# Last output tile of an attention-and-ReGLU kernel: blocks of 256, 128, 64 and 64 columns from a ring of six PSUM banks

## Chip, cores, metric

One core of one Trainium2 chip. The metric is the device time of one execution in microseconds.

## The reference

```python
# x: 8 x 8 x 512 x 64, state: 8 x 8 x 32 x 64 (batch, head, rows, depth), float32
scores = x @ state^T / 8;  a  = softmax(scores);   xread = a @ state
scores2 = state @ x^T / 8; a2 = softmax(scores2);  sread = a2 @ x
y = concatenate([xread, sread], axis=rows)      # 8 x 8 x 544 x 64
t = y.transpose(0, 2, 1, 3).reshape(4352, 512)
out = (relu(t @ w_gate) * (t @ w_val)) @ w_out  # d_ff 1536, out 4352 x 512 float32
```

## The kernel before

Operands are bfloat16, sums are float32 in PSUM. Six banks (0 to 5) are a ring for most work, and two (6 and 7) hold output tiles in turn. An output tile has 128 rows of 512 columns and is the sum of 12 matmuls (`NF` = 12). It is copied from PSUM to one of four output buffers in SBUF and stored from there. At the very end come the two tiles of the state rows, row group 2 of the last batch and, as last tile, its row group 3, which `out_last` splits into column blocks.

```python
opool = pool("opool", 4)                # four output buffers, in turn
# ...
def bank(name, kind="r"):
    if given:
        n = given.pop(0)
    # ...
    else:
        n = turn["r"] % 6 if kind == "r" else 6 + turn["o"] % 2
        turn[kind] += 1
    return psum.tile([128, 512], FP32, name=name, tag=f"b{n}")

def o_bank():
    return bank("o_ps", "o")
# ...
def fin_x(b, tsub, eng="act"):
    o_sb = opool.tile([128, d_model], FP32, name="o_sb", tag="o_sb")
    copy[eng](out=o_sb, in_=held["o", b, tsub])
    n = 2 if b == B - 2 or (b == B - 1 and tsub == 0) else 1
    # ... n stores by SyncE
# ...
def out_last(b, tsub):
    for lo, n, eng, q in ((0, 256, nc.scalar.copy, nc.scalar), (256, 128, nc.scalar.copy, nc.scalar),
                          (384, 128, nc.vector.tensor_copy, nc.sync)):
        cols = slice(lo, lo + n)
        ps = o_bank()[:, 0:n]
        for jf in range(NF):
            nc.tensor.matmul(ps, hsb[b][:, jf, tsub * 128:(tsub + 1) * 128], wo_sb[:, jf, cols],
                             start=(jf == 0), stop=(jf == NF - 1))
        o_sb = opool.tile([128, d_model], FP32, name="o_sb", tag="o_sb")
        eng(out=o_sb[:, 0:n], in_=ps)
        q.dma_start(out=out_rows(b, tsub)[:, cols], in_=o_sb[:, 0:n])
# ...
for t2 in range(2):                      # state rows
    out_mms(hs_sb, B, t2, list(range(NF)))
    fin_s(t2)
for i in range(NF - lag % NF, NF - 3):   # row group 2 of the last batch
    out_piece(B - 1, i)
out_last(B - 1, NC - 1)
```

The softmax here doesn't subtract the row's maximum and nothing guards it: scores larger than these inputs give would overflow.

Of the kernel before, what the change touches and what calls it, by code (L numbers as in the profile page):

```python
# [16 lines left out]
def kernel(  # L17
# [9 lines left out]
    nc = tc.nc  # L27

    B, H, S, D = x.shape
# [51 lines left out]
# [4 lines that stand above are left out]
        elif kind == "spare":  # L85
            n = 6 + turn["o"] % 2
# [4 lines that stand above are left out]
# [255 lines left out]
    def o_bank():  # L346
        return bank("o_ps", "o")
# [8 lines left out]
    def out_rows(b, tsub):  # L356
        return out[b * SP: b * SP + S].rearrange("(p q) m -> q p m", q=NC)[tsub]

    def fin_x(b, tsub, eng="act"):
        o_sb = opool.tile([128, d_model], FP32, name="o_sb", tag="o_sb")  # L360
        copy[eng](out=o_sb, in_=held["o", b, tsub])  # L361
        n = 2 if b == B - 2 or (b == B - 1 and tsub == 0) else 1
        for i in range(n):
            rows = slice(128 // n * i, 128 // n * (i + 1))
            nc.sync.dma_start(out=out_rows(b, tsub)[rows], in_=o_sb[rows])
# [8 lines left out]

    def out_last(b, tsub):

        for lo, n, eng, q in ((0, 256, nc.scalar.copy, nc.scalar), (256, 128, nc.scalar.copy, nc.scalar),
                              (384, 128, nc.vector.tensor_copy, nc.sync)):
            cols = slice(lo, lo + n)
            ps = o_bank()[:, 0:n]  # L380
            for jf in range(NF):
                nc.tensor.matmul(ps, hsb[b][:, jf, tsub * 128:(tsub + 1) * 128], wo_sb[:, jf, cols],  # L382
                                 start=(jf == 0), stop=(jf == NF - 1))
# [3 lines that stand above are left out]
# [5 lines left out]
    def out_piece(b, i):  # L392
        out_part(b, i)
        if i % 3 == 2:
            fin_x(b, i // 3)
# [37 lines left out]
    def spin(n, cols=512):  # L433
        for i in range(n):
# [6 lines left out]
             "sc": att_sc, "ex": att_exp, "nr": att_sum, "nx": att_scale, "aT2": att_T2, "ao2": att_out2, "aT": att_T, "ao": att_out,  # L441
             "c": c_unit, "co": c_out, "u": u_unit, "uo": u_out, "gv": gv, "re": relu, "mu": mult, "o": out_part,
             "of": fin_x, "xn": x_next, "xp": x_pad, "sr": sr_mm, "sn": sr_norm}
    program = """
    dx.1.0.2 dx.1.1.2 stc.0.0.act stc.0.1.act xc.0.0.dve dw.0.0.128 spin.7 stT.0@4 xc.0.1.act dw.1.0.128 on xT.0.0@2
# [86 lines left out]
    for g in range(first, NF * (B + 1)):  # L532
        b, jf = divmod(g, NF)
# [14 lines left out]
    for i in range(NF - lag % NF, NF - 3):  # L548
        out_piece(B - 1, i)
    out_last(B - 1, NC - 1)  # L550


# [28 lines left out]
```

## Time and profile before

| What | Before |
|---|---|
| Time, median of the first 3 runs | 223.4 us (223.28 to 224.25) |
| Span of the profiled run, from the trace | 221.73 us |
| First matmul of the last tile (called T0 below) | 215.95 us |
| Tail: from T0 to the end of the span | 5.78 us |

The prediction shows the lines of the profile that matter and reads them. For reading them: SPq, ACTq and DVEq are the instruction queues of SyncE, ScalarE and VectorE, "landing" is the time from a store's issue to the signal that its data has arrived, and the chain that ended last is the work and waits followed back from the last instruction.

### The profile page before, as it was taken

To read this page: it belongs to the slowest core of one execution; us is meant where nothing else is said; L and a number is where in the kernel's file an instruction comes from. 1 tells how busy PE (TensorE), PEld (TensorE's weight loads), DVE (VectorE), ACT (ScalarE), POOL (GpSimd) and SP (SyncE) were. 2 spreads that over 40 slices of the span, in tenths; PEclk is the share of its full clock that TensorE was granted. 3 is DMA by queue.
4 is the path that set the end of the run, shared out by engine and by line. 5 is a ranking of instruction groups with operands and counts; after the bars stand their busy time and mean duration, and the time that the engine had idled before them with its cause. 6 is when DMAs were issued, how large, how long until landed. Compare 5 with 4: busy or idle time off the path is not lost.

```text
span 221.7 us, 4851 instructions
## 1 busy us (share of the span) xinstructions
PE 216.0 (97%) x1959; PEld 106.3 (48%) x1959; DVE 130.5 (59%) x228; ACT 124.8 (56%) x238; POOL 49.4 (22%) x54
## 2 busy tenths in 40 slices
PE   7799999999999999999999999999999999999994
PEld 3454455444554444444444444445444445666544
DVE  2697898965786569664767378646874433222100
ACT  5489888565767555564466456645654444222222
POOL 8777826460004233015000700000000000000000
PEclk9999999999999999999999999999999999999999
DMA  6999999182065962771169114501311112222332
GB/s 156 174 195 197 203 237 276 43 154 86 4 146 188 146 233 79 156 240 51 50 146 278 53 47 101 104 34 50 95 50 47 49 47 50 50 47 55 89 95 95
DMA packets 37879, 25.48 MB, mean 115 GB/s; under 512 B 18944, under 2 KB 33280, under 8 KB 37856
## 3 DMA queue, kind: packets, MB, share of 16 engines
q1 hardware_dynamic: 24992, 16.85, 28.7%
q0 software_dynamic: 11968, 7.47, 21.7%
q10 hardware_dynamic: 896, 0.85, 1.4%
q8 instruction: 15, 0.25, 0.5%
q14 instruction: 8, 0.07, 0.1%
HBM read 18.35 MB, written 8.91 MB: 123 GB/s over the span
## 4 chain that ended last, share of the span: by engine, by line
PE 85%; DMA 12%; POOL 1%; issue 0%; DVE 0%; POOLq 0%; DVEq 0%
PE o_ps L353 39%; PE gv_ps L316 32%; DMA xb<-in_x_dram 9%; PE gv_ps L333 5%; PE up L291 4%; DMA wg_sb<-in_moe_w_gate_dram 4%; PE sr_ps L264 1%; PE sc_ps L200 1%; PE o_ps L382 1%; PE xT_ps L186 0%; POOL xb L415 0%; PE stT_ps L129 0%; PE aT_ps L235 0%; PE srT_ps L277 0%; PE upc L291 0%
## 5 line engine op out<-in xcount | busy, mean ns | idle before, releaser
L353 PE MATMUL o_ps<-wo_sb,h_sb 128*128 128x512 bf16 x372 | 94.8, 379 | 0.0
L316 PE MATMUL gv_ps<-ans,U 128*128 128x512 bf16 x384 | 94.4, 379 | 0.0
L344 DVE TENSOR_TENSOR h_sb<-gv_ps,g_sb 128x512 bf16<-128x512 f32 x96 | 65.0, 689 | 43.5 <-ACT g_sb L340 42.1
L340 ACT ACTIVATE g_sb<-gv_ps 128x512 bf16<-128x512 f32 (+1 forms) x108 | 62.9, 588 | 45.9 <-PE gv_ps L316 35.0
L316 PEld LDWEIGHTS <-U 128*128 128x128 bf16 x384 | 36.1, 98 | 40.7 <-issue 0.4
L353 PEld LDWEIGHTS <-h_sb 128*128 128x128 bf16 x372 | 35.3, 98 | 39.7 <-issue 1.6
L361 ACT COPY o_sb<-o_ps 128x512 f32<-128x512 f32 x31 | 18.3, 590 | 17.4 <-PE o_ps L353 17.4
L301 ACT CAST U<-up 128x512 bf16<-128x512 f32 x36 | 18.9, 593 | 12.1 <-PE up L291 12.0
L142 POOL CAST xb<-xf 128x1024 bf16<-128x1024 f32 x10 | 10.6, 1088 | 66.4 <-DMA xf<-in_x_dram 45.4
L301 DVE CAST U<-up 128x512 bf16<-128x512 f32 x36 | 22.7, 684 | 4.1 <-PE up L291 3.7
L256 POOL COPY xa<-xb 128x2048 bf16<-128x2048 bf16 (+1 forms) x9 | 15.5, 1748 | 0.3
L213 DVE TENSOR_REDUCE cs<-e_sn 128x16 f32<-128x512 bf16 x16 | 10.9, 683 | 7.3 <-ACT e_sn L207 7.3
L344 DVE TENSOR_TENSOR hs_sb<-gv_ps,g_sb 128x256 bf16<-128x256 f32 x12 | 5.1, 425 | 15.3 <-PE gv_ps L333 10.8
L207 ACT ACTIVATE e_sn<-sc_ps 128x512 bf16<-128x512 f32 x16 | 9.6, 600 | 7.4 <-PE sc_ps L200 7.4
L219 DVE TENSOR_TENSOR a_sn<-e_sn,rc 128x512 bf16<-128x512 bf16 x16 | 12.4, 778 | 0.4
L291 PEld LDWEIGHTS <-stT 64*32 64x32 bf16 x512 | 5.9, 90 | 9.5 <-issue 8.1
L311 ACT CAST U<-upc 128x512 bf16<-128x512 f32 (+1 forms) x21 | 10.1, 570 | 0.5 <-PE upc L291 0.4
L200 PEld LDWEIGHTS <-xT 128*128 128x128 bf16 x128 | 5.7, 98 | 4.1 <-DVE xT L177 0.8
L291 PE MATMUL up<-wg_sb,stT 64*32 64x512 bf16 x144 | 7.5, 382 | 0.0
L291 PE MATMUL up<-wv_sb,stT 64*32 64x512 bf16 x144 | 7.2, 380 | 0.0
L333 PE MATMUL gv_ps<-br,wg_sb 128*128 128x256 bf16 x48 | 7.2, 273 | 0.0
L333 PE MATMUL gv_ps<-br,wv_sb 128*128 128x256 bf16 x48 | 7.2, 273 | 0.0
(63 smaller groups left out, 121.5 us busy)
## 6 DMA issues: line engine op xcount, KB each, us to landing
out_dram<-o_sb SPq DMA_DIRECT2D x26, 256.0 KB, 2.4
xf<-in_x_dram SPq DMA_DIRECT2D x4, 1024.0 KB, 6.3
wo_sb<-in_moe_w_out_dram POOLq DMA_DIRECT2D x2, 768.0 KB, 14.5
wg_sb<-in_moe_w_gate_dram POOLq DMA_DIRECT2D x5, 256.0 KB, 8.6
wv_sb<-in_moe_w_val_dram POOLq DMA_DIRECT2D x5, 256.0 KB, 10.5
out_dram<-o_sb SPq DMA_DIRECT2D x10, 128.0 KB, 2.4
xf<-in_x_dram POOLq DMA_DIRECT2D x1, 1024.0 KB, 16.1
xb<-in_x_dram POOLq DMA_DIRECT2D x3, 256.0 KB, 6.8
```

Source lines behind the costliest of these rows:

```text
L142: copy[eng](out=xb[b][:, :, hs].rearrange("p c h d -> p h c d"), in_=xf[b][:, hs])
L213: nc.vector.reduce_sum(out=cs, in_=e_v, axis=AX.X)
L219: {"dve": nc.vector, "pool": nc.gpsimd}[eng].tensor_tensor(out=by_pair(a_sn[b], jp).rearrange("p r (j n) -> p r j n", n=Ns), in0=e_v, in1= ...
L256: nc.gpsimd.tensor_copy(out=v[:, hs:hs + src.shape[1]], in_=src)
L291: nc.tensor.matmul(dst[parity][32 * j:32 * j + 32], stT[r:r + 64, b, j, 32 * parity:32 * parity + 32], wsb[r:r + 64, j, lo:lo + n], start= ...
L301: copy[eng](out=U[b][:, w, kc, lo:lo + 512], in_=held["u", b, w, lo][kc])
L316: nc.tensor.matmul(ps[w], U[b][:, w, kc, f0:f0 + 128], ANS[b][:, kc].rearrange("p c t -> p (c t)"), start=(kc == 0), stop=(kc == NK - 1))
L333: nc.tensor.matmul(ps[w][:, 0:nt], wsb[:, j, f0:f0 + 128], br[:, j].rearrange("p b n -> p (b n)"), start=(j == 0), stop=(j == NJ - 1))
L340: nc.scalar.activation(out=g_sb[:, 0:n], in_=ps[0][:, 0:n], func=AF.Relu)
L344: nc.vector.tensor_tensor(out=dst, in0=ps[1][:, 0:n], in1=held["g", b, jf][:, 0:n], op=ALU.mult)
L353: nc.tensor.matmul(held["o", b, tsub], src[:, jf, tsub * 128:(tsub + 1) * 128], wo_sb[:, jf], start=(jf == 0), stop=(jf == NF - 1))
L361: copy[eng](out=o_sb, in_=held["o", b, tsub])
```

## The change

The intent: a smaller last block gives a shorter last copy and a smaller last store. The four blocks come from the ring of six banks, so that no block waits for another's evacuation (its copy out of PSUM), and evacuations and stores are shared out. One earlier tile goes out in one store instead of two.

```diff
@@ fin_x
-        n = 2 if b == B - 2 or (b == B - 1 and tsub == 0) else 1
+        n = 2 if b == B - 2 else 1
@@ out_last
-        for lo, n, eng, q in ((0, 256, nc.scalar.copy, nc.scalar), (256, 128, nc.scalar.copy, nc.scalar),
-                              (384, 128, nc.vector.tensor_copy, nc.sync)):
+        for lo, n, eng, q in ((0, 256, nc.scalar.copy, nc.sync), (256, 128, nc.scalar.copy, nc.scalar),
+                              (384, 64, nc.vector.tensor_copy, nc.sync), (448, 64, nc.vector.tensor_copy, nc.scalar)):
             cols = slice(lo, lo + n)
-            ps = o_bank()[:, 0:n]
+            ps = bank("o_ps")[:, 0:n]
```

## The prediction

> **What bounds the kernel now.** I read the page first: busy shares and slices, then the chain that ended last. After that I read the pieces of that chain in the last microseconds, the instructions of the same stretch in order of time, and the landing times of the stores. The page says:
>
> ```profile
> PE 216.0 (97%) x1959; PEld 106.3 (48%) x1959; DVE 130.5 (59%) x228; ACT 124.8 (56%) x238; POOL 49.4 (22%) x54
> ...
> PEclk9999999999999999999999999999999999999999
> ...
> PE 85%; DMA 12%; POOL 1%; issue 0%; DVE 0%; POOLq 0%; DVEq 0%
> ```
>
> TensorE is busy for 97% of the span at full clock, and the chain is TensorE for 85%. Nothing but fewer or faster matmuls, or a shorter start or end, can move the time. The change touches only the end (and one store before it), so the end is all that needs sizing. The chain in order of time, from 205 us on, closes like this (start, duration, what):
>
> ```profile
> 207.48 8.63 PE o_ps L353 x40
> 216.11 2.67 PE o_ps L382 x36
> 218.78 0.04 DVEq L385
> 218.81 0.04 issue
> 218.85 0.29 DVE o_sb L385
> ```
>
> The 36 matmuls of the last tile follow the earlier ones without a gap, and the last block's evacuation on VectorE is the last work. The instructions of the tail in order of time (start, duration, engine, line; in brackets the idle time before and what ended it):
>
> ```profile
> 215.95 2.81 PE L382 MATMUL o_ps<-wo_sb,h_sb 128*128 128x256 bf16 x36
> 216.15 0.59 ACT L361 COPY o_sb<-o_ps 128x512 f32<-128x512 f32 x1 [2.00 <-PE o_ps L353]
> 216.76 0.35 SPq L365 DMA_DIRECT2D out_dram<-o_sb  x1
> 217.46 0.37 ACT L385 COPY o_sb<-o_ps 128x256 f32<-128x256 f32 x1 [0.72 <-PE o_ps L382]
> 217.86 0.36 ACTq L386 DMA_DIRECT2D out_dram<-o_sb  x1
> 218.39 0.27 ACT L385 COPY o_sb<-o_ps 128x128 f32<-128x128 f32 x1 [0.56 <-PE o_ps L382]
> 218.69 0.36 ACTq L386 DMA_DIRECT2D out_dram<-o_sb  x1
> 218.85 0.29 DVE L385 COPY o_sb<-o_ps 128x128 f32<-128x128 f32 x1 [10.84 <-PE o_ps L382]
> 219.17 0.35 SPq L386 DMA_DIRECT2D out_dram<-o_sb  x1
> ```
>
> The span ends at 221.7. After the last matmul that makes 0.07 us to the copy, 0.29 of copy, 0.03 to the store, and 2.56 from the start of the store's issue (219.17) to the end. The stores of this stretch:
>
> ```profile
> out_dram<-o_sb SPq DMA_DIRECT2D x2, 256.0 KB, 2.0
> out_dram<-o_sb SPq DMA_DIRECT2D x5, 64.0 KB, 1.7
> out_dram<-o_sb ACTq DMA_DIRECT2D x5, 64.0 KB, 2.0
> out_dram<-o_sb ACTq DMA_DIRECT2D x1, 128.0 KB, 1.9
> ```
>
> In a view of the last microseconds alone, both 64 KB stores of the last tile land after 1.6 us. So the last one lands at about 219.17 + 1.6 = 220.77, and some 0.96 us of closing semaphores and drains follow that no part of the change touches.
>
> **What the Trainium skill says.**
>
> (1) "PSUM — Partial Sum Buffer", section "PSUM bank collisions raise a hardware error": a bank that one engine writes must not be read by another at that moment, so TensorE must wait for the evacuation before it fills the bank again. Before, the three blocks alternate between two banks. The third reuses the bank of the first, whose copy ends at 217.46 + 0.37 = 217.83, and its first matmul starts at 217.93 by narrow windows of the timeline. There was 0.1 us to spare, and the view of that line lists no idle time of TensorE. So the bank wait that the ring of six would remove is not there in the kernel before.
>
> (2) "TensorE: Matmul & The Clock Gate", section "Back-to-back issue gap", gives about 81 ns per pair of weight load and matmul at 128 columns, and about 60 cycles (25 ns) as the floor up to 64 columns. The trace disagrees on the first: the starts of the 128-column matmuls run from 217.26 to 218.54 in 23 steps, 55.7 ns each. On the second it is close: the score matmuls (64 columns, a new 128x128 weight each) take 0.40 us for eight with 193 ns for one, so (0.40 - 0.193) / 7 = 29.6 ns a step:
>
> ```profile
> 150.11 0.40 PE L200 MATMUL sc_ps<-stT,xT 128*128 128x64 bf16 x8
> ```
>
> (3) "VectorE: DVE Perf Modes", section "The TRN2 errata", puts a copy from PSUM to SBUF at 120 + columns cycles of 0.96 GHz. For 128 columns that is 258 ns and the trace shows 292, so the fixed part is larger. The slope, 1.04 ns a column, agrees with the trace: the 512-column casts from PSUM take 684 ns, (684 - 292) / 384 = 1.02.
>
> (4) "DMA: Bandwidth & Descriptors", section "Anatomy of one DMA": most of a transfer's fixed 2 us is the receipt for the last byte. (It is stated for transfers issued by GpSimd; here stores from ScalarE and SyncE show 1.6 to 2.0.) So a fixed part remains however small the last store is.
>
> **The change part by part.**
>
> *One store instead of two for row group 0 of the last batch.* It goes out well before the tail, and saves one SyncE issue of about 0.35 us on a queue that mostly waits. Off the path: 0.
>
> *Ring of six banks.* It removes a wait of 0, as shown. It is needed by the other part, though: with two banks the fourth block would reuse the second's, whose copy ends at 218.39 + 0.27 = 218.66, while TensorE would want it at about 218.29.
>
> *The last 128 columns as two blocks of 64.* Twelve matmuls and weight loads more. The first starts at 217.93. 23 steps of 29.6 ns take the last one to 218.61, and with 193 ns it ends at 218.80, against 218.78 before: +0.02 us on the path. The last copy is 64 columns: 292 - 64 x 1.02 = 227 ns, so -0.065. It would begin at 218.87 and end at 219.10; plus 0.03, its store is ready at 219.13 (before 219.17).
>
> *Queues.* Block 0's store goes to SyncE, so ScalarE has only block 1's store (218.69) and then block 3's. Block 2's copy on VectorE starts at 217.93 + 11 x 0.0296 + 0.193 + 0.07 = 218.52, ends at 218.75 and its SyncE issue begins at 218.78, beside ScalarE's. Where both queues issued side by side in the tail, two issues took 0.85 us on ScalarE and 0.81 on SyncE, so about 0.43 each instead of 0.36. ScalarE is then free at 218.69 + 0.43 = 219.12, just before 219.13. The last issue starts at about 219.13: -0.04 in sum.
>
> *The last transfer.* Its rows are 256 bytes instead of 512. The trace's records of packets have about 27 ns for one of 512 bytes and 18 ns for one of 256 (in loads; no store of that size is in the trace). There are 128 rows over 16 engines, eight on each, so 8 x 9 = about 0.07 us less. I take 1.53 instead of 1.6 to landing, an estimate.
>
> *Sum.* TensorE +0.02, copy -0.065, queue 0, transfer -0.07: about -0.11 us of 223.4, 0.05%. That makes 223.3.
>
> **The rivals.**
>
> *The weight load, not the columns, sets the pace at 64 columns.* If each pair costs 55 ns as at 128 columns, the two blocks take 1.33 us instead of 0.66: +0.6 us, less the 0.14 of copy and transfer, so about 223.9. Against it speak the 29.6 ns above; for it, that those came in runs of eight and here 24 follow one another.
>
> *A buffer wait takes over.* Four output buffers go round. Block 3's copy takes the buffer of row group 2, whose 256 KB store is issued at 216.76 and lands 2.0 us later, at 218.76. TensorE releases the copy at 218.87. That is 0.1 us of margin. If that store lands 0.3 us late, the gain is gone and 0.2 is lost: 223.6.
>
> *ScalarE's queue serialises the last two stores.* It has only 0.01 us of margin in my own sum. If an issue beside another takes longer, or a semaphore instruction stands between, the last store starts up to 0.1 us late and the sum is 0: 223.4.
>
> *Short rows are slow to write.* "DMA: Bandwidth & Descriptors", section "Specifications", wants 512 bytes or more for line rate and says that shorter transfers make the engines read and write back. No store of this trace is that short. Some 0.2 us more on the landing would leave 223.5.
>
> **Range and chances.** All paths lie between 223.2 and 223.9, while the three runs before spread from 223.28 to 224.25. The spread of the runs is wider than the effect, so the range comes mainly from it: 223.3 us, 222.8 to 223.9 eight times in ten. Two per cent are 4.5 us, more than the 2.9 us between the last matmul and the end, so no shortening of that tail can give them. A loss of that size would take a stall that nothing here suggests. Chances: faster 0.01, within 2% 0.98, slower 0.01.
>
> **What the changed profile would show.** Right: the last matmul's end at about 218.8, the 64-column matmuls in steps near 30 ns, VectorE copies of about 227 ns with the last starting near 218.87 after a wait on TensorE, ScalarE's last issue beginning at about 219.13 directly after its one before, and a landing near 1.5 us. Wrong step by step: matmul steps of 55 ns (weight load rival); VectorE's last copy released by a store (buffer rival); a gap between the last copy's end and ScalarE's issue of over 0.05 us (queue rival); a landing of 1.7 us or more (short rows). The prediction as a whole would be wrong if TensorE showed idle time ahead of the last tile, or if the body before 215 us moved by more than the runs' spread.

## The result

| | Before | Changed |
|---|---|---|
| Time, median of 6 runs | 223.76 us (223.28 to 224.25) | 223.57 us (223.23 to 224.3) |
| Ratio | | 0.9996, 95% interval 0.9972 to 1.002 |
| Span of the profiled run | 221.73 us | 222.17 us |
| T0 | 215.95 us | 216.49 us |
| Last copy starts, from T0 | 2.90 us | 3.02 us |
| Last store's issue starts, from T0 | 3.22 us | 3.27 us |
| From there to the end | 2.56 us | 2.41 us |
| Tail | 5.78 us | 5.68 us |

A ratio is the mean time of one kernel's runs over that of the other's in the same rounds, so it is not quite the ratio of the medians.

The profiled run of the changed kernel has the longer span, although its tail is 0.1 us shorter. The 0.54 us come from before T0. In the page of the changed kernel, the second fortieth of the span (5.6 to 11.1 us) ran at a granted clock (the share of full speed that TensorE was allowed) of 0.6 to 0.7:

```profile
PEclk9699999999999999999999999999999999999999
```

From an early landmark on, the two runs agree again. The state reads of the first two batches (64 matmuls of one line) start at these times in the lists by time, first before, then changed:

```profile
43.69 0.71 PE L264 MATMUL sr_ps<-xa,e_sn 128*32 128x65 bf16 x64
```

```profile
44.23 0.70 PE L264 MATMUL sr_ps<-xa,e_sn 128*32 128x65 bf16 x64
```

T0 follows 172.26 us later in both (215.95 - 43.69 and 216.49 - 44.23). In all thirteen profiles the distance is 172.26 to 172.45 us, while the landmark itself lies between 42.93 and 44.36. So nearly all of the spread between runs arises in the first 43 us, which the change does not touch, and it is 1.4 us wide. (The low clock is not shown to be its cause: the latest landmark, 44.36, belongs to a run at full clock.) Whole times cannot resolve a tenth of a microsecond here, but the tail counted from T0 can. Every reading below is such a tail; as a difference of rounded times it can be off by 0.01 us.

The tail of the changed kernel, in order of time; "x2" joins two stores of one queue, and the seconds of each pair start at 219.32 (SPq) and 219.76 (ACTq):

```profile
216.49 2.84 PE L382 MATMUL o_ps<-wo_sb,h_sb 128*128 128x256 bf16 x48
...
218.00 0.37 ACT L385 COPY o_sb<-o_ps 128x256 f32<-128x256 f32 x1 [0.72 <-PE o_ps L382]
218.39 1.26 SPq L386 DMA_DIRECT2D out_dram<-o_sb  x2
218.67 0.27 ACT L385 COPY o_sb<-o_ps 128x128 f32<-128x128 f32 x1 [0.30 <-PE o_ps L382]
218.96 1.16 ACTq L386 DMA_DIRECT2D out_dram<-o_sb  x2
219.07 0.22 DVE L385 COPY o_sb<-o_ps 128x64 f32<-128x64 f32 x1 [10.52 <-PE o_ps L382]
219.51 0.22 DVE L385 COPY o_sb<-o_ps 128x64 f32<-128x64 f32 x1 [0.21 <-PE o_ps L382]
```

The matmuls end at T0 + 2.84, but the last copy starts only at T0 + 3.02. The list names TensorE as the releaser. The chain that ended last names another:

```profile
217.30 2.04 DMA out_dram<-o_sb
219.33 0.04 DVEq L385
219.37 0.05 issue
219.42 0.05 DVEq L385
219.47 0.04 issue
219.51 0.22 DVE o_sb L385
```

The chain runs through the 256 KB store of row group 2, issued at 217.30 and landed at 219.34, then through two semaphore instructions on VectorE's queue (DVEq), to the copy. The fourth block takes the output buffer that this store reads. The last three stores, kilobytes and microseconds to landing:

```profile
out_dram<-o_sb ACTq DMA_DIRECT2D x1, 64.0 KB, 1.6
out_dram<-o_sb SPq DMA_DIRECT2D x1, 32.0 KB, 1.5
out_dram<-o_sb ACTq DMA_DIRECT2D x1, 32.0 KB, 1.5
```

### The profile page after: what moved, and what is told of

Its sections match the earlier page's. It is cut to its first block, busy times and chain, and to the rows that moved or that the text cites. A ratio compares the mean times of both kernels' runs of the same rounds, so it can differ in the third digit from the quotient of the medians. Undisturbed runs are those within 1.5% of the kernel's fastest.

```text
span 222.2 us, 4878 instructions
## 1 busy us (share of the span) xinstructions
PE 216.5 (97%) x1971; PEld 106.6 (48%) x1971; DVE 130.0 (59%) x229; ACT 124.7 (56%) x238; POOL 48.9 (22%) x54
## 4 chain that ended last, share of the span: by engine, by line
PE 94%; DMA 4%; ACT 0%; issue 0%; POOL 0%; DVE 0%; DVEq 0%; POOLq 0%
PE o_ps L353 39%; PE gv_ps L316 38%; PE gv_ps L333 5%; PE up L291 4%; DMA xb<-in_x_dram 3%; PE sc_ps L200 2%; PE upc L291 2%; PE sr_ps L264 1%; PE xT_ps L186 1%; PE warm_ps L435 1%; DMA out_dram<-o_sb 1%; PE aT_ps L235 1%; PE xT_ps L173 0%; PE stT_ps L129 0%; ACT o_sb L361 0%
## 5 line engine op out<-in xcount | busy, mean ns | idle before, releaser
L219 DVE TENSOR_TENSOR a_sn<-e_sn,rc 128x512 bf16<-128x512 bf16 x16 | 11.7, 734 | 0.4
L435 PE MATMUL warm_ps<-hs_sb 128*128 128x512 bf16 x15 | 6.3, 535 | 1.2 <-DVE hs_sb L399 1.2
```

What stands on the lines that cost most here:

```text
L219: {"dve": nc.vector, "pool": nc.gpsimd}[eng].tensor_tensor(out=by_pair(a_sn[b], jp).rearrange("p r (j n) -> p r j n", n=Ns), in0=e_v, in1= ...
```

## The experiments

Theory: the last copy is held 0.14 us by its buffer, and the smaller last store lands earlier. These two and the shorter copy make the tail. Rivals: the copy is held by TensorE or by VectorE's own queue; the earlier end comes from the queue of the last store; the bank ring or the moved first store brings the gain. Eleven runs followed: nine new kernels, one of them twice, and the changed kernel again. All gave correct results.

### A buffer of its own for the fourth block

```diff
-            o_sb = opool.tile([128, d_model], FP32, name="o_sb", tag="o_sb")
+            if lo == 448:
+                o_sb = const.tile([128, 64], FP32, name="o_own")
+            else:
+                o_sb = opool.tile([128, d_model], FP32, name="o_sb", tag="o_sb")
```

(More buffers of full size do not fit: two more were asked for, with room for four in all, and that kernel did not build.)

> The changed kernel, but its fourth block is copied into a small buffer of its own instead of the one that the store of row group 2 still reads. Measured from the first matmul of the last tile (T0) in the profile: before, last copy starts at 2.90 us, last store at 3.22, span ends at 5.78; changed, 3.02, 3.27 and 5.68. Buffer-wait theory: the last copy starts at 2.91 (TensorE's last end 2.84 plus 0.07), the last store at about 3.16 and the span ends at about 5.57. Rival (VectorE is held by its semaphores between the two copies, or by TensorE): the copy stays at 3.02 and the end at 5.68. Whole time within 0.3% of the changed kernel either way.

Measured: T0 at 215.42, last copy at T0 + 2.88, last store at 3.14, tail 5.56. Time 222.75 in one look, beside 223.92 of before.

```profile
218.30 0.22 DVE L388 COPY o_own<-o_ps 128x64 f32<-128x64 f32 x1
218.56 0.36 ACTq L389 DMA_DIRECT2D out_dram<-o_own  x1
```

The 222.75 us are 0.4% under the changed kernel's 223.57, a little outside the expected 0.3%. With the buffer wait gone, the copy starts 0.14 us earlier and the end comes 0.12 us earlier. The two semaphore instructions went with the wait, so this run alone does not part the two; the next one moves the landing. The chain that ended last now goes from TensorE straight to this copy. The buffer theory predicted the end within 0.01 us, and the rival predicted no move. The 1.2 us in the single look is the spread of the start (the timed repeat is below).

### Three output buffers: the wait made larger

```diff
-    opool = pool("opool", 4)
+    opool = pool("opool", 3)
```

> The changed kernel with three output buffers instead of four: the suspected wait made larger. The fourth block then takes the buffer of the first block, whose 128 KB store is issued at T0 + 1.90 and lands 1.9 us later. Buffer-wait theory: the last copy starts at about T0 + 3.8 to 4.0 (changed: 3.02), and the span ends 0.8 to 1.0 us later relative to T0, at about 6.5 to 6.7. Rival: end at 5.68 as in the changed kernel.

Measured: last copy at T0 + 4.17, tail 6.86. The buffer wait is now that for the first block's store. In the chain that ended last:

```profile
217.36 1.88 DMA out_dram<-o_sb
...
219.53 0.05 DVEq L385
...
219.63 0.23 DVE o_sb L385
```

The wait scales as the theory says, but it overshot my range by 0.2 us. The store landed at 219.24 and the copy started 0.39 us later, with four semaphore instructions of VectorE in that gap of the chain. In the changed kernel there were two, in 0.17 us. The third block's copy was held as well: with three buffers it takes the one of row group 2, whose store landed at T0 + 2.84, and it started at T0 + 3.25, 0.41 us later. So, as an estimate from these gaps, each semaphore instruction that stands between the landing and the copy costs about 0.1 us.

### Four blocks on the two old banks

```diff
-            ps = bank("o_ps")[:, 0:n]
+            ps = o_bank()[:, 0:n]
```

> The changed kernel with its four blocks on the two old banks in turn. If the bank ring is needed by the fourth block: TensorE finds the second block's bank busy until its copy ends (T0 + 2.18 + 0.27 = 2.45) and its last block starts 0.1 to 0.2 us late (before T0 + 2.33); since the last copy waits for a buffer until 3.02 anyway, only 0.05 to 0.1 us of it reach the end: span end at T0 + 5.7 to 5.8. Rival (the ring is worth nothing even with four blocks): T0 + 5.68 and no TensorE wait.

Measured: the 48 matmuls take 3.01 us instead of 2.84, the last copy starts at T0 + 3.10, and the tail is 5.78:

```profile
215.62 3.01 PE L382 MATMUL o_ps<-wo_sb,h_sb 128*128 128x256 bf16 x48
```

Without the ring, the fourth block starts 0.17 us late, and the tail's whole gain is gone. So the ring is needed by the fourth block. There is a lesson on reading here too: the view of the matmuls' line lists no idle time of TensorE for this run either. The ends of matmuls are modelled in the profile, and here a wait of 0.17 us went unlisted, so an empty list does not show that there was none. The chain that ended last does show it. The fourth block's 12 matmuls are a piece of their own, which starts just after the end of the second block's copy (217.80 + 0.27 = 218.07):

```profile
215.78 2.33 PE o_ps L382 x36
218.11 0.00 issue
218.11 0.53 PE o_ps L382 x12
```

### The ring alone, in the kernel before

```diff
-            ps = o_bank()[:, 0:n]
+            ps = bank("o_ps")[:, 0:n]
```

> The kernel before with its three blocks from the ring of six banks and nothing else. Prediction's claim (no bank wait in the kernel before): last tile's matmuls take 2.81 us, last copy at T0 + 2.90, end at T0 + 5.78, all within 0.03. Rival (a hidden wait for the first block's bank): matmuls 0.05 to 0.1 us shorter and the end earlier by as much. It is also a second look at how much the tail of one and the same program varies.

Measured: matmuls 2.81 us, last copy at T0 + 2.90, last store at 3.23, tail 5.78; each within 0.01 of before. With three blocks the ring is worth nothing. Here the tail repeats to a hundredth; where the same kernel was profiled twice (below), the two tails agree within 0.02 us.

### The first store moved to SyncE, in the kernel before

```diff
-        for lo, n, eng, q in ((0, 256, nc.scalar.copy, nc.scalar), ...
+        for lo, n, eng, q in ((0, 256, nc.scalar.copy, nc.sync), ...
```

> The kernel before, with the store of its first block moved from ScalarE to SyncE and nothing else. ScalarE is free earlier: the copy of the second block starts at T0 + 2.18 instead of 2.44. Off-path theory: the last block's copy (2.90), the last store (3.22) and the end (5.78) stay where they are within 0.03. Rival (the second block's late evacuation held something that ends last): end 0.1 to 0.25 us earlier.

Measured: the second block's copy at T0 + 2.18 instead of 2.44, last copy at 2.91, tail 5.76. Before, ScalarE's copy waited behind its own store issue: that issue ended at T0 + 2.27 (217.86 + 0.36), and the copy began 0.17 us later, behind two semaphore instructions. This is ring_only first, which still has that order, then this run:

```profile
218.42 0.27 ACT L385 COPY o_sb<-o_ps 128x128 f32<-128x128 f32 x1 [0.56 <-PE o_ps L382]
```

```profile
218.66 0.27 ACT L385 COPY o_sb<-o_ps 128x128 f32<-128x128 f32 x1 [0.30 <-PE o_ps L382]
```

From their T0 (215.98 and 216.48) these are 2.44 and 2.18. The view charges both idles to TensorE, but the matmuls are the same, and only the store is gone from ahead of the copy. So 0.26 us of ScalarE's time were freed, off the path: at most 0.02 us reach the end.

### Three blocks of 256, 192 and 64 columns

```diff
-        for lo, n, eng, q in (..., (256, 128, nc.scalar.copy, nc.scalar),
-                              (384, 64, nc.vector.tensor_copy, nc.sync), (448, 64, nc.vector.tensor_copy, nc.scalar)):
+        for lo, n, eng, q in (..., (256, 192, nc.scalar.copy, nc.scalar),
+                              (448, 64, nc.vector.tensor_copy, nc.sync)):
```

> The changed kernel with blocks of 256, 192 and 64 columns: the same last block but only three buffers taken, so no wait on the store of row group 2; the last store is issued by SyncE. Buffer-wait theory: last copy at T0 + 2.9, store at 3.15, end at about 5.57. If the shorter end of the changed kernel comes from the last store's queue (ScalarE) rather than from its size, the issue-to-end stretch is 2.56 us as before; if from the size, 2.41 as in the changed kernel.

Measured: last copy at T0 + 2.90 and last store at 3.15, as expected without the buffer wait, but 2.70 us from there to the end: tail 5.85, longer than before. The stores:

```profile
out_dram<-o_sb ACTq DMA_DIRECT2D x1, 96.0 KB, 1.8
out_dram<-o_sb SPq DMA_DIRECT2D x1, 32.0 KB, 1.7
```

The 32 KB took 1.7 us instead of 1.5. By the trace's packet records, its packets overlap in time with those of the 96 KB store, issued 0.31 us before it, for 0.16 us; in the kernels before and changed the packets of the last two stores lie apart. This run alone left two readings: the store ahead, or a last store from SyncE being slower. The next one tests the second.

### The queues of the last two stores swapped, fourth block in its own buffer

```diff
-                              (384, 64, nc.vector.tensor_copy, nc.sync), (448, 64, nc.vector.tensor_copy, nc.scalar)):
+                              (384, 64, nc.vector.tensor_copy, nc.scalar), (448, 64, nc.vector.tensor_copy, nc.sync)):
```

> The fourth block in a buffer of its own, and the queues of the last two stores swapped: third block's store by ScalarE, fourth's by SyncE. Times from the first matmul of the last tile (T0). With the last store on ScalarE (buffer of its own) it was issued at 3.14 and the span ended 2.42 us after. Size theory (a 32 KB store of 64 columns lands earlier whichever engine issues it): last store at about 3.13, end 2.4 us after it, T0 + 5.55. Queue theory (a last store from SyncE ends later): end 2.56 to 2.7 us after its issue, T0 + 5.7 to 5.85. Contention theory for the run with three blocks (2.72 us there, because its 96 KB store was still moving): here the store before is 32 KB and nearly done, so again 2.4.

Measured: last store at T0 + 3.14 by SyncE, 2.45 us to the end, tail 5.59.

```profile
219.11 0.33 SPq L389 DMA_DIRECT2D out_dram<-o_own  x1
```

SyncE's 32 KB store lands in 1.5 us too. So the shorter end comes from the size of the last store, not from its queue: from its issue to the end it is 2.41 to 2.47 us in every run with 32 KB but three_blocks, and 2.53 to 2.56 in the three with 64 KB. The 2.70 us with three blocks stay open. Overlap alone does not explain them: in this run too the packets of the last two stores overlap for 0.16 us, with a store of 32 KB ahead instead of 96. By the packet records the last packet of the last store ended 1.14 us after the issue with three blocks and 1.11 here. What grew is the time from that packet to the landing, 0.56 us against 0.41 (0.37 where nothing overlaps). The size of the store ahead was not varied alone.

### One block of 512 columns, in the kernel before

```diff
-        for lo, n, eng, q in ((0, 256, nc.scalar.copy, nc.scalar), (256, 128, nc.scalar.copy, nc.scalar),
-                              (384, 128, nc.vector.tensor_copy, nc.sync)):
+        for lo, n, eng, q in ((0, 512, nc.scalar.copy, nc.sync),):
```

> The kernel before with its last tile in one block of 512 columns: the splitting undone, to size what it is worth as a whole. Worked out from the durations of the kernel before: last matmul's end at 11 x 0.2165 + 0.38 = T0 + 2.76, ScalarE copy of 0.59 from 2.80, store at 3.41, landing 2.0 us later and 0.96 of closing: T0 + 6.37, that is 0.6 us more than before. If the end were set by a fixed time alone, whatever the size of the last block, it would be T0 + 5.8.

Measured: copy at T0 + 2.79, store at 3.40, tail 6.47. That is 0.10 us more than worked out; the store landed after 2.03 us, and 1.05 instead of 0.96 us followed.

```profile
219.60 0.58 ACT L384 COPY o_sb<-o_ps 128x512 f32<-128x512 f32 x1 [2.00 <-PE o_ps L381]
220.21 0.35 SPq L385 DMA_DIRECT2D out_dram<-o_sb  x1
```

Splitting the tile as the kernel before does had already won 0.69 us (6.47 - 5.78). The change could only add to what was left: from T0 + 2.8, where the matmuls end in every version without a bank wait, to the end, most of it a store's landing and the close.

### The last block by ScalarE; the buffer of its own and the changed kernel, timed

```diff
-        ..., (256, 128, nc.scalar.copy, nc.scalar),
-                              (384, 64, nc.vector.tensor_copy, nc.sync), (448, 64, nc.vector.tensor_copy, nc.scalar)):
+        ..., (256, 128, nc.vector.tensor_copy, nc.sync),
+                              (384, 64, nc.vector.tensor_copy, nc.sync), (448, 64, nc.scalar.copy, nc.scalar)):
```

with the fourth block in its own buffer as above.

> Candidate from the experiments: four blocks, the fourth in a buffer of its own and evacuated and stored by ScalarE; the second and third block go by VectorE and SyncE. From T0: third block's copy at 2.58 on VectorE; last matmul's end 2.84, ScalarE copy from 2.87, 0.21 us (0.266 less 64 columns at 0.83 ns), last store at 3.10, and 2.42 to 2.5 us to the end (the third block's store is issued at 2.89, so the two may overlap): T0 + 5.52 to 5.6, against 5.78 before and 5.68 changed. Rival (VectorE and its handover to ScalarE cost nothing): 5.56 as with the buffer of its own alone. In time: 0.2 us less than before, 0.1%, verdict same; the spread of the runs comes from the first 43 us.

> The kernel whose fourth block has a buffer of its own, again and now timed. From T0: last copy 2.88, last store 3.14, end 5.56, each within 0.02 of the first look if what follows the first 43 us is fixed. In time: 0.2 us less than before (0.1%), so the verdict is same; a single look had shown 1.2 us less (222.75 against 223.92), which by this theory was the start's spread and will not repeat.

> The changed kernel itself, on the same chip as the two others. From T0: last copy 3.02, last store 3.27, end 5.68, each within 0.02. In time: 0.1 us less than before, 0.05%, verdict same, with the interval wider than the effect. If the second look's tail differs by more than 0.05 us, readings of the tail at that size are not to be trusted.

| Kernel | Last copy | Last store | Tail | Median of 6 runs | Ratio to before, 95% interval |
|---|---|---|---|---|---|
| scalar_last | T0 + 2.88 | 3.12 | 5.59 | 223.59 us | 1.0012 (0.9995 to 1.003) |
| own_buffer_timed | 2.88 | 3.14 | 5.56 | 222.98 us | 0.9987 (0.9973 to 1.0001) |
| changed_again | 3.02 | 3.27 | 5.70 | 223.62 us | 1.0021 (0.9998 to 1.0044) |

Before had a median of 223.28 us of 11 runs (222.72 to 223.94). The tails repeat: 5.56 twice, and 5.68 and 5.70. ScalarE's copy took 0.21 us and its store started 0.02 us earlier:

```profile
219.03 0.21 ACT L388 COPY o_own<-o_ps 128x64 f32<-128x64 f32 x1 [1.00 <-PE o_ps L382]
219.27 0.36 ACTq L389 DMA_DIRECT2D out_dram<-o_own  x1
```

However, it took 2.47 us to the end instead of 2.42 (its store landed in 1.6 us, the other's in 1.5), so nothing is won. The third block's store, issued 0.14 us ahead of it on SyncE (0.30 in own_buffer_timed), may be the reason: the packets of the two overlap for 0.17 us here and lie apart there. That was not tested alone.

The whole times do not follow the tails: 0.1 and 0.2 us less than before were expected of changed_again and scalar_last, and both medians are 0.3 us more. The changed kernel's tail differs from its first look by 0.02 us, within the 0.05 set beforehand. The changed kernel had one run of 224.68 us at a granted clock of 0.992, and scalar_last two (223.82 and 224.06), where all 11 runs of before and all six of own_buffer_timed were at 0.998 or more. The low clock is not all of it: the other runs still spread by about 1 us. The version with a buffer of its own has the shortest tail of all and the lowest median, but its interval reaches 1.0001, so in time it is not shown to be faster.

## Why the prediction was right

The time was within 0.3 us of the predicted 223.3, and the verdict is the one it gave 98%. Its frame was right as well: the change acts on the tail alone, and there it forecast -0.11 us and -0.10 was measured. That these two agree so closely is luck: the last copy's wait and the end of the last store were both mis-sized, and the errors cancelled. By the prediction's own sign (a last copy released by a store) the buffer rival came true.

- *Ring of six banks, removed wait 0; needed by the fourth block.* Right on both (ring_only 0.00, two_banks +0.10 on the tail of the changed kernel). The argument from an empty list of idle time was weaker than it looked.
- *Last 128 columns as two blocks.* Right: the matmuls ended at T0 + 2.84 (2.85 forecast), the copies took 224 ns (227), the third block's copy started at T0 + 2.58 (2.57). The weight load rival fell: by the trace's records the 24 matmuls of 64 columns start 29.1 ns apart, one after another.
- *"TensorE releases the copy at 218.87. That is 0.1 us of margin."* This is the step that failed. The rival of the buffer wait happened in part: the landing was as forecast (T0 + 2.85 against 2.81 in the prediction's times), but two semaphore instructions on VectorE stood between landing and copy, 0.17 us, where the sum had 0.07 from TensorE's last matmul to the copy. The copy started at T0 + 3.02, where 2.92 was forecast. The margin was also read too large: it set the landing (218.76) against the start of the copy (218.87). TensorE's end in the same sum is 218.80, which leaves 0.04 us.
- *Queues.* The sum said that ScalarE would be free just in time, 0.01 us before it was needed. That kept block 1's store at its old time, and missed that ScalarE's own issue of block 0's store had held the copy of block 1 by 0.26 us. In the changed kernel ScalarE's first store starts at T0 + 2.47, not 2.74, and the queue had more than 0.4 us to spare. So its last issue did not follow directly on the one before, though that was forecast.
- *The last transfer, -0.07.* The term itself was right and something was left out. The stretch from the last store's issue to the end fell from 2.56 to 2.41 us, -0.15. By the packet records the last packet ended 1.13 us after the issue instead of 1.20, -0.07 as forecast (a packet of 256 bytes took 18 ns, one of 512 bytes 27). The time from the last packet to the landing, which the sum took as fixed, fell too, from 0.42 to 0.37 us, -0.05. The remaining -0.02 came after the landing and is not there in the second look. The short-rows rival fell: rows of 256 bytes did not land later.
- *Sum.* Last store's issue +0.05 instead of -0.04, and from there to the end -0.15 instead of -0.07: together -0.10 instead of -0.11.
- *One store instead of two for an earlier tile, 0.* It was not isolated in a run. The distance from the landmark to T0 is the same 172.26 us before and after. The second look at the changed kernel has 172.39, so an effect of up to about 0.1 us there could not be seen.

## What to carry to other kernels

When a tail is split further, count the output buffers along with the banks: a fourth block that takes the buffer of a store still in flight pays for the landing and then for each semaphore instruction behind it, and a small buffer of its own gave that back here. A smaller last store ended sooner in eight of nine runs; in the ninth it was issued 0.31 us behind one of 96 KB, so look at the store ahead as well. Before hunting for tenths, find a landmark from which runs repeat, and measure from there, because a noisy start can be ten times the effect.

## What the Trainium skill lacked or had wrong

- "TensorE: Matmul & The Clock Gate", section "Back-to-back issue gap": it gives about 81 ns per pair of weight load and matmul at 128 columns. Here 24 such pairs ran at 55.7 ns each, and eight at 64 columns, each with a new weight of 128 columns, at 29.6 ns. The 55.7 ns are close to the 56 ns that the section gives for a matmul alone and calls an under-count in a stream of pairs.
- "DMA: Bandwidth & Descriptors", section "Anatomy of one DMA": it has a fixed 2.0 us, fitted for transfers issued by GpSimd. Stores from ScalarE and SyncE landed after 1.5 us for 32 KB, 1.6 for 64, 1.9 for 128 and 2.0 for 256, and the page has no such times for stores from these two engines.
- The same page, section "Specifications": transfers under 512 bytes are said to be read and written back. Stores of 256-byte rows landed in 1.5 us, sooner than those of 512-byte rows. Their packets took 18 ns each against 27, less per packet and more per byte; whether anything was read and written back is not shown.
- The same page, section "Issuing engines are not separate DMA queues": it calls the time to initiate a transfer usually small beside the transfer. Here an issue took 0.36 us beside 1.6 to landing, and it held ScalarE's next copy by 0.26 us, which the section does not mention.
- I found no page with what semaphore instructions on an engine's queue cost once a transfer has landed: two of them went with 0.17 us on VectorE, four with 0.39. The nearest is the time in which a sequencer reads a semaphore's value, in "Advanced Engine Details and Errata".
